# Attention and expert layer on one core: transfers in halves, three at a time, and a scheduler with other costs

## The chip, the core and the metric

The kernel runs on one core of a Trainium2 chip. The metric is the time of one execution on the device in microseconds. The core has a matrix engine (PE, whose weight loads the profile lists as PEld), a vector engine (DVE), an activation engine (ACT), a general engine (POOL) and a sync engine (SP), which here issues nearly all transfers between HBM and the on-chip memory SBUF. Matrix products land in PSUM, which has eight banks. Each engine works through its own list of instructions in order.

## The reference

```python
q_rot, k_rot = (rotate(q), rotate(k))          # 8 batches, 8 heads, 576 rows, 64 columns
scores = scale * np.matmul(q_rot, k_rot.transpose(0, 1, 3, 2))
scores = scores - np.max(scores, axis=-1, keepdims=True)
attn = np.exp(scores)
attn = attn / (np.sum(attn, axis=-1, keepdims=True) + 1e-09)
x = np.matmul(attn, v)                         # then heads side by side: x is (8, 576, 512)
...
scores = np.einsum('bsd,d->bs', x, w_gate)
for b in range(B):
    top_idx = np.argpartition(-scores[b], capacity)[:capacity]     # the 128 best rows of a batch
    xe = x[b, top_idx]
    ye = np.maximum(xe @ w1, 0.0) @ w2                             # 512 to 1024 to 512
    g = 1.0 / (1.0 + np.exp(-scores[b, top_idx]))
    out[b, top_idx] = x[b, top_idx] + g[:, None] * ye              # all other rows are x
```

## The kernel before

Two heads make a pair; four pairs make a batch; there are 32 pairs. For a pair SP loads `k_in` (576 KB), `q_in` (640 KB) and two halves of v in `vt` (576 KB each, v stands four times in it), by `load` (L443) and `load_v` (L459). `k_in` and `q_in` have three buffers, `vt` four (two pairs). POOL rotates k and q by four instructions (`rotate`, L469; the first pair is rotated by DVE). PE multiplies q by k in nine units of 64 or 128 rows, two matmuls each, into two banks per unit (`units`, L508). DVE takes the negative maximum of each row (`nm`), ACT the exponential with the row's sum (`prob`, `sums`), DVE transposes `prob` in 32 x 32 blocks, and PE multiplies by v in two halves of 144 small matmuls (`value`, L556). The result goes through `ot`, is turned by five transposes on PE and is scaled by 1/sum into `x`, on ACT by ten instructions or on DVE by two (`scaled`, L612).

Two pairs fill one half of a batch's `x`. `half_done` (L654) stores it (512 KB and 64 KB), multiplies it by the gate's weights on POOL (`prod`) and sums that up on ACT or DVE (`gp`). `route` (L693) makes the scores `sc`, spreads them over columns by five transposes on PE, counts on DVE how many rows rank ahead (`cnt`, `rank`), and `chosen` selects 128 rows (`sel`), gathers them (`xe`) by an indirect DMA, after which `experts_of` multiplies by `w1t` and `w2t` and scatters the result. The weights' four pieces each (512 KB a piece) are loaded after the products of pairs 0 to 3 (`weights`, L889).

What runs when isn't written by hand. Every step is an `Op` with a key and with durations for the engines that may do it, and `Order.run` (L110) plays through the whole kernel with these numbers: whenever an engine is free, it gets the waiting step with the smallest key whose inputs and banks are there. `issue` (L239) then writes the instructions out in that order. So durations, costs of switching PE between kinds of products (`SWITCH`, `STAY`), the choice of banks (`Banks.take`) and the numbers in `KEY` decide the order of every engine's list, SP's too, but not how long anything takes on the chip. All engine instructions are recorded by one helper, so the profile puts them on one line, L222, and tells them apart by their tiles.

Of the kernel before, what the change touches and what calls it, by code (L numbers as in the profile page):

```python
# [18 lines left out]
P = 128  # L19
# [3 lines left out]
KEY = dict(lag=44704, value=6306, rows=-177, load=43737, rotate=14014, half=1424, gate=72760, route=862,  # L23
           count=116221, select=-5108, turn=109130, step=-36115, hold=2, patience=1011, over=71, narrow=5,
           s01=7594, s02=628, s10=736994, s12=-866157, s20=21404, s21=450)
# [18 lines left out]
class Banks:  # L44
# [13 lines left out]

    def take(self, kind, t):
        f = self.free  # L60
        if kind == "quad":
            i = 0
        elif kind == "wide":
            i = min((max(f[i], f[i + 1]) > t, i < 4, max(f[i], f[i + 1]), i) for i in range(0, self.n, 2))[3]
# [13 lines left out]
class Op:  # L78
    __slots__ = ("engines", "fn", "key", "banks", "waits", "outs", "ready", "start", "end", "done", "mode", "seq", "urgent",
                 "moved")  # L80


class Order:
# [9 lines left out]
    def op(self, engines, fn, key, after=(), bank=None, mode=0, urgent=False, moved=0):  # L93

        o = Op()
        o.moved = moved
# [13 lines left out]
    def run(self):  # L110
# [4 lines left out]
        mode, shared, wire = 0, 0.0, 0.0  # L115
# [13 lines left out]
        while events:  # L129
# [4 lines left out]
            while moved:  # L134
                moved = False
                for e in names:
# [56 lines left out]
                    free[e] = begin + takes  # L193
                    heapq.heappush(events, free[e])
# [44 lines left out]
def issue(tc, nc, order):  # L239

    needs = {}
# [3 lines left out]
    made, last = {}, {}  # L245
# [44 lines left out]
def attention_moe_kernel(ctx: ExitStack, tc: tile.TileContext, q, k, v, w_gate, w1, w2, rope, outs, cap):  # L290
# [152 lines left out]
    def load(pi):  # L443
# [5 lines left out]
        def dma(n, dst, src, use, late, moved):  # L449
            o = op(LOAD, lambda: nc.sync.dma_start(dst, src), key + late, use.before, moved=moved)  # L450
# [3 lines left out]
        for n, use, src, cuts in ("k", kin, k, KCUTS), ("q", qin, q, QCUTS):  # L454
            for i, (lo, hi) in enumerate(zip(cuts, cuts[1:]) if pi == 0 else [(0, cuts[-1])]):
                dma(n, use.tile[:, :, lo:hi], src[b, j, :, :, lo:hi], use, 2 * i + (n == "q"), 8 * P * (hi - lo))
        loaded[pi] = (kin, qin, got)

    def load_v(pi):  # L459
        b, j = divmod(pi, NP)  # L460
        vals[pi] = []
        for i in range(2):
            use, src = vts.next(), v[b, j, :, i * NB // 2:(i + 1) * NB // 2]
            o = op(LOAD, lambda use=use, src=src: nc.sync.dma_start(use.tile, src),
                   at(pi, 0) - KEY["load"] + 5 + i, use.before, moved=8 * P * NB // 2 * D)
            use.by(o)
            vals[pi].append((use, o))
# [32 lines left out]
    def attend(pi):  # L500
# [7 lines left out]
        def units(us, key):  # L508
# [16 lines left out]
            o = op(pe(2 * M288 + 24 * (len(us) - 1)), products, key, needs + room, bs,  # L525
# [30 lines left out]
        def value(key, late):  # L556
# [17 lines left out]
            for i in range(2):  # L574
                o = op(pe(NB // 2 * 280), lambda i=i: products(i), key, turned + [got[i], o], acc, mode=1)
# [19 lines left out]
            gd = op({"ACT": act(9, 60.0)}, guarded, key, list(exps.values()) + rs.before)  # L595
            rr = op({"DVE": dve(9, 1, 60.0)}, lambda: nc.vector.reciprocal(r, r), key, [gd])
# [23 lines left out]
            g = op({"DVE": dve(4 * P), "ACT": act(4 * P, 7 * 40.0)},  # L620
# [4 lines left out]
            g_ = op({"DVE": dve(P), "ACT": act(P, 40.0)},  # L625
# [28 lines left out]
    def half_done(b, i, key):  # L654
# [4 lines left out]
        s0 = op(STORE, lambda: nc.sync.dma_start(outs[b][0:512, cs].rearrange("(p t) m -> p t m", t=NT), x.tile[:, 0:4, :]),  # L659
                key, made, moved=4 * P * NT * DM // 2)  # L660
        s1 = op(STORE, lambda: nc.sync.dma_start(outs[b][512:S, cs], x.tile[0:REM, 4, :]), key, made,
                moved=2 * REM * DM)
# [3 lines left out]
        for t0, t1 in () if b == B - 1 and i else ((0, 2), (2, 4), (4, 5)):  # L666
# [16 lines left out]
            o = op({"DVE": dve((t1 - t0) * DM // 2), "ACT": act((t1 - t0) * DM // 2, (t1 - t0) * 247.0 - 40.0)},  # L683
# [5 lines left out]
        x.by(s0, s1)  # L689
        stored += [s0, s1]  # L690
# [309 lines left out]
```

## Time and profile before

| | us |
|---|---|
| median of 3 runs | 618.16 (614.37 to 623.51) |
| profiled execution | 617.93 |
| its span, first to last instruction | 616.2 |
| PE busy | 536.7 (87%) |
| DVE busy | 469.6 (76%) |
| ACT busy | 353.8 (57%) |
| POOL busy | 353.4 (57%) |

97.91 MB pass the DMA engines in the span, 159 GB/s on average. The granted PE clock is 0.983 of full speed on average. In rows of the trace PE products are named by what they read: `k_in,q_in` is q times k, `prob,vt` the value product, `ident,...` a transpose, `xt,w1t` and `w2t,ht` the experts. "Idle before" with a releaser is time in which that engine stood still until the named engine's work ended; "issue" there means that nothing the profile shows was waited for.

### The profile page before, as it was taken

What the parts mean: (1) busy time and instruction counts of PE and PEld (TensorE: products, weight loads), DVE (VectorE), ACT (ScalarE), POOL (GpSimd) and SP (SyncE); (2) the same over time, 40 slices, a digit from 0 to 9 for tenths busy, and PEclk for the clock granted to TensorE, in tenths of its full rate; (3) what the DMA queues carried; (4) which work ended last, traced back from release to release, by engine and by line L of the source; (5) the groups of instructions that cost most, each with busy time, mean ns of one, the idle gap of its engine ahead of it and who ended that gap; (6) DMA issues with size and microseconds to landing.
All of it is one profiled execution on the core that took longest, in us unless ns stands there. A gap on an engine that the chain in (4) does not pass through costs nothing.

```text
span 616.2 us, 25530 instructions
## 1 busy us (share of the span) xinstructions
PE 536.7 (87%) x11280; PEld 386.5 (63%) x11280; DVE 469.6 (76%) x849; ACT 353.8 (57%) x1121; POOL 353.4 (57%) x271
## 2 busy tenths in 40 slices
PE   4777977787879998899988999899988999899996
PEld 2445755565657755677567675577566775577673
DVE  6967877979889967898679876899578976895420
ACT  3555756655766655665665745666566656763300
POOL 2948586457666835577553938568464867122110
PEclk9899898999989999899999999999998999999999
DMA  8756655453635464253555444454654534230110
GB/s 322 279 196 260 211 194 183 161 161 135 210 118 190 161 213 165 90 173 131 197 178 195 165 124 148 144 183 155 215 176 139 164 117 176 81 118 21 40 52 17
DMA packets 32974, 97.91 MB, mean 159 GB/s; under 512 B 3040, under 2 KB 14048, under 8 KB 32864
## 3 DMA queue, kind: packets, MB, share of 16 engines
q1 hardware_dynamic: 31040, 91.50, 43.4%
q0 software_dynamic: 1280, 4.20, 2.0%
q8 instruction: 88, 1.44, 0.9%
q10 hardware_dynamic: 544, 0.59, 0.3%
q14 instruction: 22, 0.18, 0.1%
HBM read 84.74 MB, written 11.53 MB: 156 GB/s over the span
## 4 chain that ended last, share of the span: by engine, by line
PE 56%; DVE 15%; ACT 11%; issue 8%; POOL 5%; DMA 4%; POOLq 0%; DVEq 0%; SPq 0%
PE banks L222 56%; ACT prob L222 7%; DVE nm L222 7%; DVE prob L222 6%; DMA k_in<-k_dram 4%; ACT x L222 3%; POOL k_in L222 2%; POOL q_in L222 1%; POOL prod L222 1%; DVE junk L222 1%; ACT row L222 0%; DVE k_in L222 0%; POOL out_dram L222 0%; ACT prod L222 0%; DVE q_in L222 0%
## 5 line engine op out<-in xcount | busy, mean ns | idle before, releaser
L222 ACT ACTIVATE prob<-banks,nm 128x576 f32<-128x576 f32 x288 | 211.2, 739 | 166.2 <-DVE nm L222 165.6
L222 DVE TENSOR_REDUCE nm<-banks 128x1 f32<-128x576 f32 x288 | 204.0, 747 | 65.4 <-PE banks L222 62.7
L222 PE MATMUL banks<-k_in,q_in 64*128 64x288 f32 (+1 forms) x1152 | 207.2, 451 | 36.6 <-ACT prob L222 19.0
L222 DVE STREAM_TRANSPOSE prob<-prob 128x1152 f32<-128x1152 f32 (+1 forms) x160 | 194.6, 1236 | 22.3 <-ACT prob L222 22.3
L222 PE MATMUL banks<-prob,vt 32*64 32x160 f32 (+1 forms) x9216 | 189.0, 295 | 25.7 <-issue 16.3
L222 PEld LDWEIGHTS banks<-prob,vt 32*64 32x64 f32 x9216 | 161.7, 131 | 57.8 <-issue 35.2
L222 PEld LDWEIGHTS banks<-k_in,q_in 64*128 64x128 f32 (+1 forms) x1152 | 118.5, 198 | 103.6 <-ACT prob L222 30.5
L222 POOL TENSOR_TENSOR k_in<-k_in,tabk 128x1152 f32<-128x1152 f32 x31 | 81.5, 2628 | 158.2 <-DMA k_in<-k_dram 125.0
L222 POOL TENSOR_TENSOR q_in<-q_in,tabq 128x1280 f32<-128x1280 f32 x31 | 89.9, 2901 | 0.8 <-DMA q_in<-q_dram 0.8
L222 POOL TENSOR_TENSOR prod<-x,wg 128x512 f32<-128x512 f32 (+1 forms) x45 | 48.8, 1102 | 38.8 <-DVE x L222 22.5
L222 PEld LDWEIGHTS banks<-xt,w1t 128*128 128x128 f32 x512 | 59.4, 192 | 7.3 <-issue 5.7
L222 PE MATMUL banks<-xt,w1t 128*128 128x128 f32 x512 | 63.9, 280 | 0.0
L222 PE MATMUL banks<-w2t,ht 128*128 128x512 f32 x128 | 60.6, 602 | 0.8 <-ACT ht L222 0.6
L222 ACT ACTIVATION_READ_ACCUMULATOR prob<-banks,nm 128x1 f32 x288 | 57.5, 200 | 0.0
L222 POOL TENSOR_TENSOR q_in<-q_in 128x640 f32<-128x640 f32 x31 | 47.8, 1543 | 0.1
L222 ACT ACTIVATE x<-banks,rs 128x64 f32<-128x64 f32 (+1 forms) x196 | 42.8, 328 | 6.0 <-PE banks L222 5.5
L222 POOL TENSOR_TENSOR k_in<-k_in 128x576 f32<-128x576 f32 x31 | 43.7, 1410 | 0.0
L222 ACT COPY ot<-banks 64x64 f32<-64x64 f32 (+1 forms) x93 | 27.4, 328 | 21.1 <-PE banks L222 20.8
L222 ACT ACTIVATE prod<-prod 128x256 f32<-128x256 f32 (+1 forms) x70 | 28.5, 408 | 17.0 <-POOL prod L222 16.9
L222 DVE TENSOR_SCALAR_CACHE_REDUCE junk<-row,sc 128x128 bf16<-128x128 f32 (+8 forms) x72 | 36.2, 528 | 1.3 <-ACT row L222 1.1
L222 PEld LDWEIGHTS banks<-w2t,ht 128*128 128x128 f32 x128 | 22.2, 190 | 22.7 <-issue 19.6
L222 PE MATMUL banks<-ident,ot 128*128 128x128 f32 (+1 forms) x160 | 23.6, 279 | 8.5 <-ACT prob L222 8.5
(61 smaller groups left out, 204.0 us busy)
## 6 DMA issues: line engine op xcount, KB each, us to landing
vt<-v_dram SPq DMA_DIRECT2D x64, 576.0 KB, 4.8
q_in<-q_dram SPq DMA_DIRECT2D x31, 640.0 KB, 7.3
k_in<-k_dram SPq DMA_DIRECT2D x31, 576.0 KB, 6.1
out_dram<-x SPq DMA_DIRECT2D x16, 512.0 KB, 3.4
w1t<-w_dram SPq DMA_DIRECT2D x4, 512.0 KB, 6.6
w2t<-w_dram SPq DMA_DIRECT2D x4, 512.0 KB, 7.4
out_dram<-x SPq DMA_DIRECT2D x16, 64.0 KB, 3.0
tabk<-rope_dram ACTq DMA_DIRECT2D x2, 288.0 KB, 4.3
```

The costliest lines, as they stand in the source:

```text
L222: i = made(*args, **kwargs)
```

## The change

Loads of k and q after the first two pairs, of v after the first pair, and of the weights are cut in halves, and the main store in two. These, and the small store, are marked `alone`. In the written program each of them waits until the third before it has landed; in the scheduler's play SP isn't free for another step before that time either. Besides, `KEY`, `SWITCH` and several durations have other numbers, and the choice of banks has two new settings.

```diff
-KEY = dict(lag=44704, value=6306, rows=-177, load=43737, rotate=14014, half=1424, gate=72760, route=862,
+KEY = dict(tnear=2, wnear=0, lag=47626, value=10910, rows=18240, load=16004, rotate=-168669, half=-4551,
...
-SWITCH = ((0.0, 175.0, 194.0), (151.0, 0.0, 196.0), (151.0, 125.0, 0.0))
+SWITCH = ((0.0, 95.0, 196.0), (200.0, 0.0, 200.0), (150.0, 260.0, 0.0))
+DEPTH = 3
...
+    def far(self, i, near):
+        return near < 2 and (i < 4) != (near == 1)
...
-            i = min((i < 4, f[i ^ 1] <= t, f[i], i) for i in range(self.n) if f[i] <= t)[3]
+            i = min((self.far(i, KEY["tnear"]), f[i ^ 1] <= t, f[i], i) for i in range(self.n) if f[i] <= t)[3]
...
+                    if o.alone:
+                        free[e] = max(free[e], landed[-1] + self.SEM)
+                        landed = [o.end] + landed[:-1]
...
+        if o.alone:
+            if len(transfers) >= DEPTH:
+                tc.add_manual_dep(
+                    mine[0], transfers[-DEPTH], mybir.DependencyInfo(mybir.DependencyClass.Sync, mybir.DependencyReason.DATA),
+                    reason="transfers at a time")
+            transfers.append(mine[-1].name)
...
-            for i, (lo, hi) in enumerate(zip(cuts, cuts[1:]) if pi == 0 else [(0, cuts[-1])]):
+            for i, (lo, hi) in enumerate(zip(cuts, cuts[1:]) if pi == 0 else ()):
                 dma(n, use.tile[:, :, lo:hi], src[b, j, :, :, lo:hi], use, 2 * i + (n == "q"), 8 * P * (hi - lo))
+            for i in range(2 if pi else 0):
+                dma(n, use.tile[:, i], src[b, j, :, i], use, 2 * (n == "q") + i, 4 * P * cuts[-1])
...
+            for n, (c0, c1) in enumerate(((0, NB // 4), (NB // 4, NB // 2))):
+                o = op(LOAD, lambda use=use, src=src, cs=slice(c0, c1): nc.sync.dma_start(use.tile[:, cs], src[:, cs]),
+                       at(pi, 0) - KEY["load"] + 5 + 2 * i + n, use.before, moved=8 * P * (c1 - c0) * D, alone=pi > 0)
...
-            g = op({"DVE": dve(4 * P), "ACT": act(4 * P, 7 * 40.0)},
+            g = op({"DVE": dve(4 * P), "ACT": (8 * 205, 8 * 205 + 120)},
...
-            o = op({"DVE": dve((t1 - t0) * DM // 2), "ACT": act((t1 - t0) * DM // 2, (t1 - t0) * 247.0 - 40.0)},
+            o = op({"DVE": dve((t1 - t0) * DM // 2), "ACT": act((t1 - t0) * DM // 2, (t1 - t0) * 160.0 - 20.0)},
```

On SP, around the second pair's products, the list before has whole transfers (a name is tile and buffer, the shape is what lands in SBUF):

```order
L222 DMA k_in0_78<-k_dram 128x1152
L222 DMA q_in0_75<-q_dram 128x1280
L222 DMA w1t_120<-w1_dram 128x1024
L222 DMA w2t_121<-w2_dram 128x2x512
L222 DMA vt0_81<-v_dram 128x1152
L222 DMA w1t_120<-w1_dram 128x1024
L222 DMA w2t_121<-w2_dram 128x2x512
L222 DMA vt1_82<-v_dram 128x1152
```

and the list of the change, from the same load of `k_in0` on:

```order
L233 DMA k_in0_78<-k_dram 128x576 x2
L233 DMA q_in0_75<-q_dram 128x640 x2
L233 DMA vt0_81<-v_dram 128x512
L233 DMA vt0_81<-v_dram 128x640
L233 DMA w1t_120<-w1_dram 128x512 x2
L233 DMA w2t_121<-w2_dram 128x512
L233 DMA vt1_82<-v_dram 128x512
L233 DMA vt1_82<-v_dram 128x640
L233 DMA w2t_121<-w2_dram 128x512
```

Each transfer is now two, a group of weights (the first stands further ahead) follows v's first half instead of leading it, and v's second half goes between the pieces of w2.

On PE, where the scores of batch 3 are transposed (`sc`), the list before has this between the value products of two pairs (one row of q times k with x4 is two units):

```order
L222 MATMUL banks_63<-k_in0_78,q_in0_75 128x288 x4
L222 MATMUL banks_63<-ident_64,sc0_106 128x128 x5
L222 MATMUL banks_63<-ident_64,ot0_88 128x128 x4
L222 MATMUL banks_63<-ident_64,ot0_88 64x128
L222 MATMUL banks_63<-k_in0_78,q_in0_75 128x288 x10
```

and the list of the change, at the same scores:

```order
L233 MATMUL banks_63<-k_in0_78,q_in0_75 128x288 x4
L233 MATMUL banks_63<-ident_64,sc0_106 128x128 x5
L233 MATMUL banks_63<-w2t_121,ht0_103 128x512 x2
L233 MATMUL banks_63<-ident_64,ot0_88 128x128 x4
L233 MATMUL banks_63<-ident_64,ot0_88 64x128
L233 MATMUL banks_63<-w2t_121,ht0_103 128x512 x2
L233 MATMUL banks_63<-k_in0_78,q_in0_75 128x288 x4
L233 MATMUL banks_63<-w2t_121,ht0_103 128x512 x2
L233 MATMUL banks_63<-k_in0_78,q_in0_75 128x288 x4
L233 MATMUL banks_63<-w2t_121,ht0_103 128x512 x2
L233 MATMUL banks_63<-k_in0_78,q_in0_75 128x288 x4
```

The four pieces of the second expert product stood one pair earlier before and are now spread between these; two of q times k more come here as well.

## Rows read from the trace of the kernel before

**Rows 1.** The page: engines' busy time (share), and the chain that ended last.

```profile
PE 536.7 (87%) x11280; PEld 386.5 (63%) x11280; DVE 469.6 (76%) x849; ACT 353.8 (57%) x1121; POOL 353.4 (57%) x271
PE 56%; DVE 15%; ACT 11%; issue 8%; POOL 5%; DMA 4%; POOLq 0%; DVEq 0%; SPq 0%
```

**Rows 2.** Busy time in stretches: length, engines (instructions), PE clock, DMA share, GB/s.

```profile
20.00:180.00 160.00, 123.76 (x3008) 89.55 (x3008) 130.21 (x212) 100.61 (x322) 109.86 (x72) 0.96 0.56 190
180.00:570.00 390.00, 362.03 (x8012) 263.65 (x8012) 314.05 (x548) 237.11 (x760) 230.29 (x178) 0.99 0.45 151
570.00:616.20 46.20, 39.99 (x224) 27.36 (x224) 11.83 (x58) 7.64 (x21) 5.12 (x9) 1.00 0.10 36
```

**Rows 3.** Waits of PE from 0 to 180 us: total, times, longest.

```profile
PE banks L222 <- ACT prob L222: 17.8, 22, 2.3
PE banks L222 <- issue: 12.8, 7, 2.9
...
PE banks L222 <- ACT x L222: 3.4, 3, 1.8
```

**Rows 4.** The page's DMA queues: packets, MB, share of 16 engines.

```profile
q8 instruction: 88, 1.44, 0.9%
```

**Rows 5.** Timeline of SP, 30 to 38 us: start, duration, what it issued.

```profile
30.92 0.34 SPq L222 DMA_DIRECT2D vt<-v_dram  x1
31.30 0.43 SPq L222 DMA_DIRECT2D w1t<-w_dram  x1
31.78 0.43 SPq L222 DMA_DIRECT2D w2t<-w_dram  x1
```

**Rows 6.** Timeline of PE, 28 to 38 us; in brackets the idle time before.

```profile
37.49 0.49 PE L222 MATMUL banks<-prob,vt 32*64 32x160 f32 x6 [2.88 <-issue]
```

**Rows 7.** DMA traffic from 31.8 to 35.2 us, and from 35.2 to 37.5.

```profile
DMA packets 278, 1.11 MB, mean 325 GB/s; under 512 B 21, under 2 KB 21, under 8 KB 278
...
q8 instruction: 1, 0.02, 2.7%
```

**Rows 8.** Timeline of SP, 300 to 420 us.

```profile
328.56 0.33 SPq L222 DMA_DIRECT2D k_in<-k_dram  x1
```

**Rows 9.** Timeline of POOL, 336 to 350 us.

```profile
336.25 2.64 POOL L222 TENSOR_TENSOR k_in<-k_in,tabk 128x1152 f32<-128x1152 f32 x1 [9.30 <-DMA k_in<-k_dram]
...
346.26 1.54 POOL L222 TENSOR_TENSOR q_in<-q_in 128x640 f32<-128x640 f32 x1
```

**Rows 10.** Timeline of PE, 346 to 350 us.

```profile
348.58 1.67 PE L222 MATMUL banks<-k_in,q_in 64*128 64x288 f32 x10
```

**Rows 11.** The page's DMA issues: count, KB each, median us to landing.

```profile
k_in<-k_dram SPq DMA_DIRECT2D x31, 576.0 KB, 6.1
...
out_dram<-x SPq DMA_DIRECT2D x16, 64.0 KB, 3.0
```

**Rows 12.** Timeline of PE at the scores of batch 3, and of batch 4.

```profile
316.61 0.76 PE L222 MATMUL banks<-ident,sc 128*128 128x128 f32 x5
...
318.90 1.24 PE L222 MATMUL banks<-k_in,q_in 128*128 128x288 f32 x4 [0.99 <-ACT prob L222]
320.90 1.24 PE L222 MATMUL banks<-k_in,q_in 64*128 64x288 f32 x8 [0.76 <-ACT x L222]
...
324.59 2.73 PE L222 MATMUL banks<-prob,vt 32*64 32x160 f32 x144 [1.01 <-ACT prob L222]
...
387.29 0.76 PE L222 MATMUL banks<-ident,sc 128*128 128x128 f32 x5
```

**Rows 13.** Groups by shape: count, busy us, mean ns, idle before and its releaser.

```profile
L222 DVE TENSOR_TENSOR x<-banks,rs 128x512 f32<-128x512 f32 x14 | 9.4, 674 | 0.0
L222 DVE TENSOR_REDUCE gp<-prod 64x1 f32<-64x256 f32 x5 | 2.1, 411 | 8.7 <-POOL prod L222 8.7
L222 DVE TENSOR_TENSOR x<-banks,rs 64x128 f32<-64x128 f32 x6 | 1.6, 273 | 8.2 <-PE banks L222 8.2
```

**Rows 14.** Timeline of PE at the end.

```profile
570.57 2.05 PE L222 MATMUL banks<-xt,w1t 128*128 128x128 f32 x16
...
577.72 1.88 PE L222 MATMUL banks<-w2t,ht 128*128 128x512 f32 x4
579.44 0.27 PE L222 MATMUL banks<-ident,sc 128*128 128x128 f32 x1
```

More of the change, by code (lines that the diff above doesn't have):

```diff
@@ L79 @@
     __slots__ = ("engines", "fn", "key", "banks", "waits", "outs", "ready", "start", "end", "done", "mode", "seq", "urgent",
-                 "moved")
+                 "moved", "alone")
 class Order:
@@ L91, in __init__, with op @@
         self.ops, self.slots = [], slots
-    def op(self, engines, fn, key, after=(), bank=None, mode=0, urgent=False, moved=0):
+    def op(self, engines, fn, key, after=(), bank=None, mode=0, urgent=False, moved=0, alone=False):
         o = Op()
-        o.moved = moved
+        o.moved, o.alone = moved, alone
         o.urgent = urgent
@@ L114, in run @@
         free = {e: 0.0 for e in names}
-        mode, shared, wire = 0, 0.0, 0.0
+        mode, shared, wire, landed = 0, 0.0, 0.0, [0.0] * (DEPTH - 1)
         waiting = {e: [] for e in names}
@@ L244, in issue @@
             needs.setdefault(id(n), []).append(o)
-    made, last = {}, {}
+    made, last, transfers = {}, {}, []
     for _, _, o, e in order:
@@ L449, in dma @@
         def dma(n, dst, src, use, late, moved):
-            o = op(LOAD, lambda: nc.sync.dma_start(dst, src), key + late, use.before, moved=moved)
+            o = op(LOAD, lambda: nc.sync.dma_start(dst, src), key + late, use.before, moved=moved, alone=pi > 1)
             use.by(o)
@@ L463, in load_v @@
             use, src = vts.next(), v[b, j, :, i * NB // 2:(i + 1) * NB // 2]
[L464 to L467, printed above, removed]
+            got = []
+            for n, (c0, c1) in enumerate(((0, NB // 4), (NB // 4, NB // 2))):
+                o = op(LOAD, lambda use=use, src=src, cs=slice(c0, c1): nc.sync.dma_start(use.tile[:, cs], src[:, cs]),
+                       at(pi, 0) - KEY["load"] + 5 + 2 * i + n, use.before, moved=8 * P * (c1 - c0) * D, alone=pi > 0)
+                got.append(o)
+            use.by(*got)
+            vals[pi].append((use, got))
     def rotate(pi):
@@ L593, in guarded @@
                 nc.scalar.add(r[0:64, U:U + 1], su[64:128, 8:9], EPS)
-            gd = op({"ACT": act(9, 60.0)}, guarded, key, list(exps.values()) + rs.before)
-            rr = op({"DVE": dve(9, 1, 60.0)}, lambda: nc.vector.reciprocal(r, r), key, [gd])
+            gd = op({"ACT": (320, 425)}, guarded, key, list(exps.values()) + rs.before)
+            rr = op({"DVE": dve(9, 1, 20.0)}, lambda: nc.vector.reciprocal(r, r), key, [gd])
             sums.by(gd)
@@ L624, in value @@
                    key + late, [f, rr] + x.before, b)
-            g_ = op({"DVE": dve(P), "ACT": act(P, 40.0)},
+            g_ = op({"DVE": dve(P), "ACT": (2 * 205, 2 * 205 + 120)},
                     lambda e: scaled(e, x.tile[0:REM, 4:5, cs].rearrange("p t (h d) -> p t h d", h=2),
@@ L779, in select @@
                         sel.tile[:, t, :], slots[:, r0 // P], rank.tile[:, t:t + 1], None, op0=ALU.is_equal)
-        s = op({"DVE": dve(P, 5, 350.0), "POOL": (5 * (60 + 2.38 * P), 5 * (60 + 2.38 * P))}, select, key, [rk_] + sel.before)
+        s = op({"DVE": dve(P, 5, 350.0), "POOL": (5 * 589, 5 * 589)}, select, key, [rk_] + sel.before)
         rank.by(s)
@@ L843, in part @@
                         nc.tensor.matmul(bank_of(bank)[:, out], lhs, rhs, start=first, stop=last)
-                o = op(pe(sum(max(T32, M512 / 2 * (m[0].stop - m[0].start) / 512) * 2 for m in mms)), part,
+                o = op(pe(sum(max(T32 + 4, M512 / 2 * (m[0].stop - m[0].start) / 512) * 2 for m in mms)), part,
                        key + (step // 2 if i else 0), needs + [o], bank)
```

36 lines of the change are left out of this document (22 added, 14 removed).

## The prediction, on record before the change was run

> **What bounds the kernel now.** I began with the page's chain of waits: over half of it is PE and 8% is "issue", time in which nothing that the profile shows was waited for [rows 1]. PE's matmul order is therefore the thing to follow, and the question is where it stands still. The busy times by stretch answer that [rows 2]: between 180 and 570 us PE is busy 362.03 of 390 us (93%), DVE 314.05 (81%); between 20 and 180 us PE is busy 123.76 of 160 (77%) and DVE 130.21 (81%), so neither bounds that stage and PE stands for 36 us. The last 46 us are a chain of routing and experts. PE's waits before 180 us [rows 3] name the parts: softmax results (ACT prob) 17.8 us, "issue" 12.8 us in 7 stops, ACT's scaling of the output rows (ACT x) 3.4 us.
>
> What is an "issue" stop? The queue table has an instruction queue that moved 1.44 MB in 88 packets [rows 4], about 16 KB each; PE and its weight loads are 22,560 instructions, 256 to a packet, so these are PE's program arriving in blocks over the same DMA engines as the data. Now the longest stop: SP issues a v load, a w1 piece and a w2 piece within 0.9 us, 576 + 512 + 512 = 1600 KB by the page's sizes [rows 5]; PE stops in the middle of a value product, 6 matmuls short, and goes on at 37.49 after 2.88 us [rows 6]. Between 31.8 and 35.2 us data alone moved, 278 packets at 325 GB/s; the one packet of the instruction queue comes in the stretch behind it [rows 7]. So the block of instructions waited for the burst to drain.
>
> **The change, part by part.** The sum goes against the profiled execution, 617.93 us (a span of 616.2 and 1.7 around it); the median of the three runs is 618.16, 0.2 above.
>
> *Transfers in halves, three at a time.* Three halves are 768 to 960 KB, typically 864. At 325 GB/s [rows 7] 1600 KB need 5.0 us to drain and 864 KB 2.7, so a block that waits behind a full burst is 2.3 us earlier. That is as long as all but the longest of the 7 stops of rows 3, and would leave 1 us or so of 12.8. Since blocks meet a load more often when the same bytes are spread out, I take **10 us** off; the ends are 0 and 12.8. This is the first 180 us alone, where the order of SP's loads changes most (first listing above): the weights' four groups are interleaved with v loads in pieces.
>
> By the Trainium skill ("DMA: Bandwidth & Descriptors", section "Queues, rings and completion order") a DMA engine goes round-robin between its queues packet by packet, and by "Runtime: NRT & Kernel Launch", section "Instruction fetch mechanics", fetching is hidden since dispatch is slower than the refill. Both speak against this term and would make it 0, 10 us more in the sum; rows 6 and 7 speak against them here, and the first rival carries them.
>
> The halves also let the rotation start sooner. A k load is issued at 328.56 [rows 8] and POOL starts on it at 336.25; POOL ends the pair's rotation at 347.80 [rows 9] and PE's first product that can use it starts at 348.58 [rows 10], 0.8 us of slack, so this path decides in some pairs: DMA is 4% of the chain [rows 1], 25 us with the first load. Both halves of k now go ahead of q. k alone, 576 KB at 325 GB/s, is 1.8 us on top of the 3.0 us that even a 64 KB store takes to land [rows 11]: 4.8 instead of 7.7. That is up to 2.9 us in about three places of the chain; POOL has the sums of the gate (prod) to do in between, so I take **3**; ends 0 and 9. In 18 of the pairs the second half of q is put behind both halves of a v load; POOL's multiplication and addition on k cover 4 us of that.
>
> *The order on PE.* Once per batch of four pairs PE has transposes of scores and output and then five units of q·k with nothing between them: stops of 0.99, 0.76 and 1.01 us [rows 12]. The change puts the second expert product there in four pieces (second listing); it does so in 5 of the 7 places, since the first two batches have no experts yet. 5 x 2.76 = 13.8 us if all is gained. But the expert work has left another pair, which now has none, and PE waits for softmax there instead: before the experts begin, from 20 to 180 us, DVE has more to do than PE [rows 2]. I take half, **7**; ends 0 and 13.8.
>
> *ACT or DVE.* The scheduler now has ACT's scaling at 8 x 205 ns and gives DVE 24 large and 32 small ones, where it had 14 and 6. DVE gains 10 x 674 + 26 x 273 ns = 13.8 us [rows 13], spread over 550 us in which it is idle for 106 [rows 2]: beside other work. PE's waits for ACT x fall, **2** of the 3.4 in rows 3 (those in the middle stage are in the term before). DVE also gets ten more sums of the gate, 15 for 5. The five cost 2.1 us of work and 8.7 us of standing still until POOL's product came [rows 13], with every row maximum queued behind them on DVE and ACT and PE behind those. Ten more at that price would be 21.6 us; but eight of them come in pairs, or stand where the product is done early, and DVE has room. I add **3**; ends 0 and 21.6.
>
> *The end.* Of the expert work that PE did after the last value product, one piece of w1 (2.05 us) and one of w2 (1.88) are now ahead of it [rows 14]: 3.9 us more before it. Behind it these two filled PE while scores were ranked, and the last transpose of scores waited for one of them, from 577.72 to 579.44; it now goes with the other four. I count **+2.5**; ends 0 and 3.9. The kernel's start has the same order of loads up to pair 1 and is taken as equal. Bank choice, switch costs and the other durations have no price but the order that they make.
>
> Sum: 617.9 - 10 - 3 - 7 - 2 + 3 + 2.5 = 601.4, say **601 us**.
>
> **Rivals.** *The stops stay.* If a block of instructions waits for something other than the amount queued (three transfers are still always ahead of it), the first term is 0: 611 us. For it: the change never empties the queue, it only shortens it. Against it: rows 5 to 7. Chance 0.14.
>
> *The stops move.* The order removes holes, and DVE, with 20 us more work and in-order waits for POOL, opens others: the third term 0 and DVE's +10 instead of +3, 601.4 + 14 = 615 us. For it: between 20 and 570 us DVE already has more to do than ACT and POOL. Chance 0.16.
>
> *Loads become the pace, slower.* SP's queue is in order, and each transfer now holds it until the third before has landed. A pair takes (387.29 - 316.61)/4 = 17.7 us [rows 12] and needs 8 halves and 1.5 stores. Three at a time do that if one lands within 17.7/9.5 x 3 = 5.6 us of its issue; from there on loads decide. The nearest rows are 3.0 us (64 KB store) and 6.1 (a k load of twice the size, beside q) [rows 11]. At 3.0 + 0.9 for its own 288 KB it is 3.9, and 70% of a pair. At 6.1 it would be 19.3 us for a pair, 1.6 more, over the 22 pairs from 180 to 570 us 35 us: 636 us. Chance 0.12. The Trainium skill ("DMA: Bandwidth & Descriptors", "Rules for kernel authors") asks for at least 1 MiB in a DMA for full bandwidth, and is on this rival's side.
>
> *Everything at its good end.* -12.8 - 9 - 13.8 - 3.4 + 0 + 0 would be 579; half of the way there from the forecast is 590. Chance 0.08.
>
> **How the numbers follow.** The forecast has the remaining 0.50, with 594 to 609 as its own range. 2% of 618 is 12.4 us, about what a measurement of this kernel can tell from no change (the three runs span 9.1 us): faster is under 605.8, slower over 630.5. Four fifths of the forecast, the good end and a little of the first two rivals are faster: 0.40 + 0.08 + 0.05 = 0.53. Slower is the third rival and a remnant, 0.13; the rest, 0.34, is within. The range reaches from 587, leaving out half of the good end, to 618, which takes in the first two rivals and leaves out the third: 0.16 outside.
>
> **What would show it.** PE's "issue" waits before 180 us at 1 to 4 us for 12.8, and none over 1 us; PE busy over 83% from 20 to 180 us. k to POOL in 5 to 6 us instead of 7.7. No stops of 0.76 us behind ACT x after the scores' transposes, and a period of four pairs of 68 to 70 us instead of 70.7. DVE busy 485 to 495 us. The same 45 us from the last value product to the end. Wrong if "issue" is still over 9 us, if POOL starts later than 7.7 us after k's issue and PE stands behind it, or if DVE stands for more than 15 us behind POOL prod.

## The result: 1.0% faster, a third of what was forecast

| | before | after |
|---|---|---|
| median of 12 runs each, us | 617.64 (614.37 to 623.51) | 611.60 (607.33 to 618.97) |
| profiled execution, its span | 617.93, 616.2 | 607.33, 605.6 |

The ratio is 0.9898 (0.9859 to 0.9937). Measured twice more, beside other kernels and on another chip, it was 0.9858 (0.9780 to 0.9936) and 0.9875 (0.9834 to 0.9917). So the change is 6 to 9 us faster, where 16.5 were forecast. Ratios set fast runs against fast runs; for e8, e9 and e11 below, on whose chip the record counts seven of the thirteen runs of the kernel before as slow, the other six would give 0.992, 0.995 and 0.976 in place of the 0.984, 0.987 and 0.968 on record. The profiled execution of after is the shortest of its twelve, 4.3 us under its median, and its difference to before, 10.6 us, is larger than that of the medians.

The profile of after, read in the order of the prediction. First the page: engines and chain (answers to [rows 1]).

```profile
PE 529.1 (87%) x11280; PEld 380.5 (63%) x11280; DVE 486.5 (80%) x898; ACT 318.8 (53%) x948; POOL 355.6 (59%) x271
PE 67%; DVE 12%; issue 9%; ACT 8%; POOL 1%; DMA 1%; POOLq 0%; SPq 0%; DVEq 0%
```

POOL and DMA have all but left the chain (1% each, for 5% and 4%), PE has 67% for 56%; "issue" has not gone down. PE's idle time is span less busy: 79.5 us before, 76.5 after. The other 7.6 of the 10.6 us are busy time of the same 11,280 products. Part of that belongs to this execution, not to the kernel. Until PE's last product the granted clock was 0.50 (1.2 GHz instead of 2.4) for 20.5 us in before and for 10.2 in after, which is worth at most 5.1 us; two later profiles of the same kernel have 23.9 us of it and PE busy 534.0 and 533.8 us, at a mean clock of 0.979, where this one has 0.989. One such stretch of after, in PE's timeline beside the same work at full clock, and its busy times (the 0.50 is the clock):

```profile
192.49 0.50 PE L233 MATMUL banks<-prob,vt 32*64 32x128 f32 x8 [1.75 <-issue]
192.92 3.90 PE L233 MATMUL banks<-k_in,q_in 64*128 64x288 f32 x16
...
265.28 2.37 PE L233 MATMUL banks<-k_in,q_in 64*128 64x288 f32 x16
```

```profile
193.10:196.30 3.20, 3.20 (x14) 2.29 (x16) 1.13 (x2) 1.18 (x4) 2.62 (x1) 0.50 0.78 217
```

PE had just stood for 1.75 us. The busy times by stretch (answers to [rows 2], columns as there):

```profile
20.00:180.00 160.00, 130.80 (x3328) 94.30 (x3328) 145.25 (x238) 94.17 (x281) 118.03 (x75) 0.98 0.67 209
180.00:570.00 390.00, 360.23 (x7746) 260.24 (x7743) 317.14 (x581) 211.24 (x639) 225.38 (x179) 1.00 0.48 147
```

Before 180 us PE gained 7 us, 82% busy for 77%. From 180 to 570 us it gained nothing: 360.23 for 362.03. Why not, its waits tell: of after from 0 to 180 us (answers to [rows 3]) ...

```profile
PE banks L233 <- ACT prob L233: 19.8, 24, 1.8
...
PE banks L233 <- issue: 6.1, 8, 1.6
...
PE banks L233 <- ACT x L233: 0.8, 2, 0.4
```

... and from 180 to 560 us, of before and then of after:

```profile
PE banks L222 <- ACT prob L222: 19.3, 28, 1.5
PE banks L222 <- issue: 4.0, 11, 1.7
PE banks L222 <- ACT x L222: 3.0, 4, 0.8
```

```profile
PE banks L233 <- issue: 17.2, 27, 2.0
PE banks L233 <- ACT prob L233: 9.8, 16, 0.8
PE banks L233 <- ACT rs L233: 1.5, 2, 0.8
PE banks L233 <- ACT ht L233: 0.7, 1, 0.7
```

The new order removed 12.5 us of standing behind ACT prob and ACT x (22.3 to 9.8) and brought 2.2 us behind other work of ACT (`rs` and `ht`). "Issue" grew by 13.2 there, so that PE stands 2.9 us more in this stage than before. PE's timeline of after, from 240 to 320 us:

```profile
242.16 1.06 PE L233 MATMUL banks<-prob,vt 32*64 32x160 f32 x46 [0.53 <-issue]
...
264.82 0.53 PE L233 MATMUL banks<-prob,vt 32*64 32x160 f32 x16 [1.97 <-issue]
...
300.51 0.76 PE L233 MATMUL banks<-ident,sc 128*128 128x128 f32 x5
301.10 1.88 PE L233 MATMUL banks<-w2t,ht 128*128 128x512 f32 x4
302.82 0.75 PE L233 MATMUL banks<-ident,ot 128*128 128x128 f32 x5
...
313.16 1.06 PE L233 MATMUL banks<-prob,vt 32*64 32x160 f32 x46 [0.53 <-issue]
```

At the scores, where [rows 12] had three holes, expert pieces follow without a gap. The three rows with "issue" are new stops. That at 264.82 is of the kind of [rows 6]: 16 matmuls short of a group's end, behind loads that SP's timeline shows just ahead of it:

```profile
258.01 1.71 SPq L233 DMA_DIRECT2D vt<-v_dram  x2
260.54 0.80 SPq L233 DMA_DIRECT2D k_in<-k_dram  x2
262.19 0.33 SPq L233 DMA_DIRECT2D q_in<-q_dram  x1
```

Which stops are blocks of the program can be counted. Take PE's instructions in the order of the trace: products, weight loads, and the hundred or so semaphore instructions among them. In all twenty profiles of this document every "issue" stop of PE over 0.55 us stands at the same place in 256, at a count of 191 to 194 past a multiple of 256. So these are beginnings of blocks. Of after's 17.2 us from 180 to 560 us 12.5 stand there, of its two later profiles' 20.4 and 22.0 us 17.8 and 19.4, and of before's 4.0 us 1.9.

The stop of 0.53 us at 242.16 and 313.16 is another. It comes once in each of five batches, 71 to 72 us apart (three more follow), ahead of the same value product and at other counts. The new order has it in every profile, 2.6 us in all, and the old order in none; what PE waits for there no row says. Blocks come back nearly as regularly: PE's 22,560 products and weight loads in eight batches are 2,820 for a batch, 11.02 blocks of 256, so a block begins at almost the same place of every batch. But one that comes late in one batch need not come late in the next: the 1.97 us of 264.82 have no like a batch later.

The rest of what the prediction looked for. A k load to POOL's start on it (answers to [rows 8, 9]), SP's timeline and then POOL's: 4.9 us, and 3.7 to 5.7 in its neighbours, for 7.7.

```profile
368.14 0.80 SPq L233 DMA_DIRECT2D k_in<-k_dram  x2
...
373.01 2.63 POOL L233 TENSOR_TENSOR k_in<-k_in,tabk 128x1152 f32<-128x1152 f32 x1 [4.44 <-DMA k_in<-k_dram]
```

DVE's groups by shape (answers to [rows 13]): no sum of the gate waits for POOL.

```profile
L233 DVE TENSOR_REDUCE gp<-prod 128x2 f32<-128x512 f32 x9 | 6.0, 672 | 0.0
L233 DVE TENSOR_REDUCE gp<-prod 64x1 f32<-64x256 f32 x6 | 2.4, 401 | 0.0
```

And the end (answers to [rows 14]): from the last output transposes of the seventh batch on, PE's timeline of before ...

```profile
511.28 0.71 PE L222 MATMUL banks<-ident,ot 128*128 128x128 f32 x5
```

... and of after:

```profile
498.40 0.77 PE L233 MATMUL banks<-ident,ot 128*128 128x128 f32 x5 [0.61 <-ACT prob L233]
...
563.88 1.98 PE L233 MATMUL banks<-w2t,ht 128*128 128x512 f32 x4
```

After's last value product ends where the last of these rows begins. From the first transposes to the last value product it was 59.3 us and is 65.5, and from there to the end 45.6 and now 41.7.

### The profile page after: what moved, and what is told of

The parts are those of the page before. It is cut to its first block, busy times and chain, and to the rows that moved or that the text cites. A ratio compares the mean times of both kernels' runs of the same rounds, so it can differ in the third digit from the quotient of the medians.

```text
span 605.6 us, 25663 instructions
## 1 busy us (share of the span) xinstructions
PE 529.1 (87%) x11280; PEld 380.5 (63%) x11280; DVE 486.5 (80%) x898; ACT 318.8 (53%) x948; POOL 355.6 (59%) x271
## 4 chain that ended last, share of the span: by engine, by line
PE 67%; DVE 12%; issue 9%; ACT 8%; POOL 1%; DMA 1%; POOLq 0%; SPq 0%; DVEq 0%
PE banks L233 67%; ACT prob L233 7%; DVE nm L233 6%; DVE prob L233 3%; DVE junk L233 2%; DMA q_in<-q_dram 1%; POOL q_in L233 1%; DVE x L233 1%; ACT x L233 0%; DVE sel L233 0%; POOL k_in L233 0%; DVE q_in L233 0%; POOLq L1023 0%; DVE k_in L233 0%; POOL xe L233 0%
## 5 line engine op out<-in xcount | busy, mean ns | idle before, releaser
L233 PE MATMUL banks<-k_in,q_in 64*128 64x288 f32 (+1 forms) x1152 | 199.8, 438 | 29.2 <-ACT prob L233 11.6
L233 PE MATMUL banks<-prob,vt 32*64 32x128 f32 (+1 forms) x9216 | 188.3, 293 | 27.2 <-issue 21.6
L233 DVE STREAM_TRANSPOSE prob<-prob 128x1152 f32<-128x1152 f32 (+1 forms) x160 | 193.2, 1234 | 11.9 <-ACT prob L233 11.9
L233 PEld LDWEIGHTS banks<-k_in,q_in 64*128 64x128 f32 (+1 forms) x1152 | 113.8, 192 | 95.8 <-ACT prob L233 31.0
L233 POOL TENSOR_TENSOR prod<-x,wg 128x512 f32<-128x512 f32 (+1 forms) x45 | 48.6, 1101 | 14.6 <-DVE x L233 12.5
L233 POOL DMA_INDIRECT out_dram<-xe,idx x8 | 8.5, 1059 | 49.2 <-DVE xe L233 48.0
L233 PE MATMUL banks<-ident,ot 128*128 128x128 f32 (+1 forms) x160 | 24.4, 282 | 13.5 <-ACT prob L233 13.2
L233 PEld LDWEIGHTS banks<-ident,ot 128*128 128x128 f32 (+1 forms) x160 | 16.1, 135 | 27.8 <-ACT prob L233 26.5
```

The costliest lines, as they stand in the source:

```text
L233: i = made(*args, **kwargs)
```

## Experiments

Three questions: where the new stops come from (the cap, v's bytes, all data, or the order), what each half of the change is worth alone, and whether a third version beats both kernels. All ratios are to the kernel before on the same chip. "Holes" are PE's waits for ACT prob and ACT x from 180 to 560 us.

**The cap and v's bytes.** e1 takes the wait away and leaves order and halves.

```diff
-            if len(transfers) >= DEPTH:
+            if len(transfers) >= 100000:
```

> The change's own order and halves, word for word, without the wait for the third transfer before. Two theories of why PE's issue stops grew from 4.7 to 17.2 us behind 180 us while they shrank from 12.8 to 6.1 us ahead of it. Theory A (spread): halves under the cap keep the data queue occupied more of the time, so more instruction blocks meet a load; without the cap, issue behind 180 us falls to 8 us or less, ahead of 180 us it rises to 10 or more, and the time is 607 to 612 us. Theory B (order): the new PE list puts value products closer together, so PE uses up its blocks faster than they come; without the cap, issue behind 180 us stays at 14 us or more and ahead of it rises to 10 or more, and the time is 613 to 620 us.

617.42 us, ratio 0.9912 (0.9872 to 0.9952). PE's waits from 180 to 560 us:

```profile
PE banks L233 <- issue: 26.2, 23, 3.0
PE banks L233 <- ACT prob L233: 10.0, 16, 0.8
```

More stops without the cap (26.2 us, for 17.2 to 22.0 in three profiles of the change), so the cap doesn't bring them; it seems to take some away. e2 and e3 load only a slice of v from the third pair on (products use what is there), in the order after and in that of before.

```diff
-cs=slice(c0, c1)
+cs=slice(c0, c1 if pi < 2 else c0 + 1)
```

> The change with v loads that bring a ninth to a quarter of their bytes from the third pair on (the rest of the tile keeps the values of an earlier pair, so the result is another); order, waits and number of transfers stay. If stops for instructions come from data ahead of them in the queue, PE's issue total falls from 23.3 to 10 us or less and the time by 8 to 14 us, to 597 to 604 us. If they come from the pace of PE's own program (a limit that no data is part of), issue stays over 18 us and the time falls by 3 us at most.

> The kernel before with v loads that bring a ninth of their bytes from the third pair on (the result is another). What all contention with v is worth in the old order: if the stops are due to data in the queue, issue falls from 18.0 to 9 us or less and the time by 6 to 12 us, to 606 to 612 us; if not, issue stays over 14 us and the time falls by 2 us at most.

e2: 611.05 us, 0.9798 (0.9739 to 0.9857), issue 20.6 us behind 180 us. e3: 616.02, 0.9898 (0.9846 to 0.9950), issue 7.8. The traces move 70.4 and 66.5 MB for 97.9, about 30% less, and that takes no stop away in either; it is not v in particular. Both are 0.6 to 1% faster than with the whole of v all the same, and these runs do not show by what.

**One half of the change at a time.** e4 has halves, cap and DEPTH in the scheduler, with the keys, switch costs, durations and bank choice of before.

```diff
-SWITCH = ((0.0, 95.0, 196.0), (200.0, 0.0, 200.0), (150.0, 260.0, 0.0))
+SWITCH = ((0.0, 175.0, 194.0), (151.0, 0.0, 196.0), (151.0, 125.0, 0.0))
...
```

> Halves, cap and the scheduler that knows of it, with the numbers, durations and bank choice of before. Theory A (spread): issue behind 180 us is 12 us or more in an order much like the old one, ahead of 180 us it is 8 or less; the time is 613 to 620 us. Theory B (order): issue behind 180 us is 7 us or less, ahead of it 8 or less; the time is 604 to 611 us, better than the whole change.

663.03 us, 1.0678 (1.0618 to 1.0737): the scheduler, played anew with the old keys, makes another order, whose holes are 38.5 us. That says nothing of halves; it shows that old keys belong to old transfers. e5 is the converse, new numbers with whole and unlimited transfers (k, q, v, weights and stores); from 60 us on its PE order is that of after.

```diff
-            for i in range(2 if pi else 0):
+            for i in range(0):
```

> The new keys, switch costs, durations and bank choice alone; transfers whole and unlimited, as before. Theory B (the new order of PE is what brings the stops behind 180 us, halves and cap take some of them away again): issue at least 25 us behind 180 us and 35 in all, as without the cap, and 616 to 622 us, so that the transfers' part of the change is worth 5 to 10 us. Theory C (halves themselves make more blocks of instructions meet a load): issue under 10 us behind 180 us, as in the kernel before, and 600 to 608 us.

642.63 us, 1.0317 (1.0239 to 1.0396). PE's waits from 180 to 560 us:

```profile
PE banks L233 <- issue: 34.5, 24, 3.5
PE banks L233 <- ACT prob L233: 11.2, 14, 3.0
```

The theory that the order brings the stops holds, and costs more than it expected; halves are not their source but what makes this order bearable. Not all of the cost is stops: against the change's profile on the same chip (a2, below) PE stands 17.4 us more in "issue" (42.2 for 24.8) and is busy 7.4 us more (541.4 for 534.0), with 40.9 us for 23.9 at a granted clock of 0.50. With e5, the change itself was run again (a2):

> The changed kernel once more, unedited, so that the three kernels beside it have it on the same chip. Both theories: ratio to the kernel before 0.985 to 0.995, PE 'issue' about 6 us before 180 us and 15 to 20 us behind it. If its issue total lies more than 6 us from the 23.3 of its first profile, single profiles can't carry differences of that size.

613.73 us, 0.9858 (0.9780 to 0.9936); issue 3.8 us before and 20.4 behind 180 us.

e8 does halves and cap alone as they ought to be done: the kernel before, row by row in its order on PE, DVE, ACT and POOL, only that each load emits two transfers in its place.

```diff
-            o = op(LOAD, lambda: nc.sync.dma_start(dst, src), key + late, ...
+            o = op(LOAD, lambda: each(*[lambda i=i: nc.sync.dma_start(dst[:, i], src[:, i]) for i in range(2)]), ...
...
+        for i in mine:
+            if len(transfers) >= CAP: tc.add_manual_dep(i, transfers[-CAP], ...)
+            transfers.append(i.name)
```

> The kernel before with its own order on every engine, row by row; only each transfer (k, q from the second pair, v, weights, stores) goes as two in the same place of SP's order, and from the third pair on each waits for the third before it. This is the first term of the prediction by itself. If halves and cap shorten the stops of any order: issue before 180 us falls from 12.8 to under 5, behind it stays near 4.7, and the time is 606 to 612 us on the first chip's scale, ratio 0.980 to 0.990. Theory I (they only repair what the new order makes; the old order has few stops to repair and meets the cap's waits): issue 13 us or more in all, ratio 0.992 to 1.005. Rival (SP held in this order): PE and POOL wait for k, q or v, ratio over 1.01.

> The same without the wait: halves alone in the old order. In the new order halves without the wait already gave most (whole transfers 642.6, halves without the wait 617.4, with it 611 to 614, on different chips). If that holds in the old order too, the ratio is within 0.007 of the run with the wait, and issue at most 4 us above it. If the wait is what counts here, issue before 180 us is 8 us or more above it.

e8: 613.70 us, 0.9844 (0.9792 to 0.9896); e9, without the cap: 614.84, 0.9868 (0.9796 to 0.9941). What the wait itself gives in this order can't be told from these two. The kernel before ran between 612.42 and 630.13 us on their chip, so what e8 is worth is read from it once more, on one chip with the change:

> Halves and cap in the old order, unedited, again: ratio 0.980 to 0.990, issue about 3 us before 180 us and 10 to 14 behind it.

> The changed kernel, unedited, beside halves and cap in the old order on the same chip. If the new order is worth the 6.5 us predicted beside the first term: 0.009 to 0.012 under the ratio of the other. If its gain is eaten by stops and by the longer end: within 0.005 of it. Issue 20 to 25 us in all.

612.27 us, 0.9859 (0.9814 to 0.9903), and the change 614.66, 0.9875 (0.9834 to 0.9917). PE's waits of e8's second run, from 0 to 180 us and from 180 to 560:

```profile
PE banks L230 <- ACT prob L230: 18.1, 25, 2.3
...
PE banks L230 <- issue: 5.6, 8, 1.8
PE banks L230 <- ACT x L230: 3.3, 3, 1.8
...
PE banks L230 <- ACT prob L230: 17.1, 25, 1.0
PE banks L230 <- issue: 7.9, 9, 1.3
PE banks L230 <- ACT x L230: 3.8, 5, 0.8
```

So halves and cap alone give what the whole change gives; the new order adds nothing that can be measured, though it has 11 us of holes less. The two profiles account for that: PE is busy 533.8 us in the change and 533.9 in e8's second run, and stands in "issue" for 27.8 us in the change and 14.3 in the other.

**Is it data?** e6 (order after) and e11 (order before) load only 32 columns of k and q from the fourth pair on, and a slice of v; e6 has halves and the wait, e11 whole transfers.

```diff
+                w = cuts[-1] if pi < 3 else 32
-                dma(n, use.tile[:, i], src[b, j, :, i], ...
+                dma(n, use.tile[:, i, :w], src[b, j, :, i, :w], ...
```

> The changed kernel, but k and q loads from the fourth pair and v loads from the third bring only a small part of their data (the products then use what earlier pairs left); orders, waits and number of transfers stay. Theory D (blocks of instructions wait behind data of any kind): from 180 to 560 us issue falls from 17.2 to under 4 us, PE busy over 95% there, 592 to 600 us. Theory P (PE in this order simply runs its program faster than blocks arrive, data or not): issue stays over 14 us, 606 to 611 us.

> The kernel before, but k and q loads from the fourth pair and v loads from the third bring only a small part of their data; order and number of transfers stay. With the thin loads in the new order (0.960) this tells what the new order alone is worth where little data stands ahead of PE's program. If the holes that the new order fills are worth the 9 to 14 us that were predicted: 606 to 612 us, ratio 0.972 to 0.983, waits for ACT prob and ACT x behind 180 us at 20 us as before. If the new order is worth nothing in itself: ratio 0.960 to 0.967.

e6: 598.61 us, 0.9600 (0.9524 to 0.9675). e11: 604.12, 0.9682 (0.9629 to 0.9735). PE's waits from 180 to 560 us, of e6 and then of e11:

```profile
PE banks L233 <- issue: 10.2, 18, 1.3
PE banks L233 <- ACT prob L233: 10.0, 16, 0.7
```

```profile
PE banks L222 <- ACT prob L222: 17.6, 26, 1.0
PE banks L222 <- issue: 6.9, 9, 1.5
PE banks L222 <- ACT x L222: 3.8, 5, 0.8
```

Both theories of e6 are half right: 7 to 12 us of the stops are data, 10 stay without it, 2.6 of them the stop that is no block's beginning. With the bytes away, the new order is 0.8% ahead of the old (5 us) by the ratios; they are of two chips and their intervals overlap, so the size isn't settled. Its holes are 11.4 us less, its stops 3.3 more, and at beginnings of blocks 7.6 for 6.9 us, nearly the same. With all the bytes they are 19.4 us in the change and 7.9 in e8's second run: data before the blocks cost the new order more than the old, and that is what eats its gain.

**Fewer bytes ahead.** e7 lets two halves be under way instead of three; e10 four quarters, the same bytes in four pieces.

```diff
-            if len(transfers) >= DEPTH:
+            if len(transfers) >= 2:
```

> The changed kernel in the same order, but a transfer waits for the second before it instead of the third: two halves under way, 576 KB at most for k or q. Theory D: a block of instructions waits behind 576 KB instead of 864, 0.9 us less at 325 GB/s; with 20 or so stops behind 180 us issue falls to 8 us or less there, and the time to 600 to 606 us. Rival (loads become the pace): 9.5 transfers in 17.7 us need one each 1.86 us, so two at a time need a landing within 3.7 us of the issue; the halves landed in 3.4 to 4.1. Then PE, DVE and POOL wait for DMA, issue falls all the same, and the time is 615 to 635 us.

> The changed kernel in its own order, with k, q and v in quarters from the third pair on and a transfer waiting for the fourth before it: 576 to 640 KB under way, as with two halves, but in four pieces. Theory D (the data ahead of a block sets the length of a stop): issue behind 180 us falls from 17 to 20 to about 14, as with two halves (13.7). Whether the pace holds: each quarter has to land in 17.7/17.5 x 4 = 4.0 us; the halves took 3.4 to 4.1 with three under way, 16 KB ones 1.8 to 2.0, so about 2.8 is expected and the first 180 us have no waits for POOL q_in beyond the one at the start. Then 604 to 611 us, ratio 0.972 to 0.985. Rival (SP's issue of twice as many transfers, or the weights' pieces between them, hold the loads up): waits for POOL q_in over 8 us before 180 us and a ratio over 0.995.

e7: 628.73 us, 1.0099 (1.0027 to 1.0171). Its issue behind 180 us is 13.7 us, but PE's waits from 0 to 180 us are

```profile
PE banks L233 <- ACT prob L233: 24.9, 19, 8.4
PE banks L233 <- POOL q_in L233: 14.0, 4, 6.5
```

In the stage where the weights come too, two at a time are too few: the prediction's third rival, there and not after. Its halves landed in 3.1 to 3.5 us, within the 3.7 that a steady pair allows. e10: 623.27, 1.0075 (1.0021 to 1.0130), issue 18.2 behind 180 us and 8.3 us behind POOL q_in before it. With 576 to 640 KB ahead as in e7, it has the stops of three halves (17.2 to 22.0 us) and not the 13.7 of e7. That speaks against the amount alone, but one profile of each is little: profiles of one program differ by as much.

**Why so few in the old order?** e12 has halves and cap only for the first ten pairs, the weights and two batches' stores (`EARLY = 10`), whole transfers after that. e13 is the kernel before with 64 small matmuls ahead, while PE waits for its first data; they were meant to move every block's start by 128 instructions.

```diff
+    for n in range(64):
+        nc.tensor.matmul(banks[0:32, 7, 0:32], ident[:, 0:32], ident[:, 0:32], start=True, stop=True)
     issue(tc, nc, order.run())
```

> The old order with halves and cap only for the first ten pairs, all weights and the first two batches' stores, that is about the first 180 us; whole transfers from there, as in the kernel before. If halves are what meets more blocks behind 180 us: issue 3 to 5 us before and 4 to 6 behind it, 8 us less than with halves throughout, ratio 0.970 to 0.978, faster than the change. Rival (the old kernel's few stops there rest on where its blocks fall against the loads, and PE now comes 5 us earlier): issue over 10 us behind 180 us, ratio 0.982 to 0.995.

> The kernel before with 64 small matmuls and their weight loads (32x32) put ahead of PE's first product, while PE waits 7.5 us for its first data anyway: every block of 256 instructions then begins 128 instructions earlier in the work, and nothing else moves. If the 4 to 5 us of issue behind 180 us rest on where the blocks begin: issue there 9 us or more, and 4 to 10 us slower (ratio 1.006 to 1.016). If the length of the bursts alone counts: issue within 3 us of 18 in all, ratio 0.996 to 1.004.

e12: 615.12 us, 0.9888 (0.9836 to 0.9941), issue 10.0 us behind 180 us, with the very loads that had 4.0 in before: its rival came true. e13: 624.00, 1.0026 (0.9992 to 1.0061), issue 11.3. But it did not move the blocks. In the trace each of the 64 calls is two products and two weight loads, 256 instructions in all, which is one whole block, and the instruction queue has 89 packets for 88 (PE's groups by shape; the page's DMA queues):

```profile
L222 PE MATMUL banks<-ident 128*32 128x32 f32 x128 | 6.4, 231 | 1.4 <-POOL ident masks.py:199 1.4
```

```profile
q8 instruction: 89, 1.46, 1.0%
```

So the blocks begin at the same products as in before. One stop in PE's timeline of before, and the same in e13's:

```profile
148.71 0.29 PE L222 MATMUL banks<-prob,vt 32*64 32x160 f32 x1 [1.20 <-issue]
```

```profile
152.91 0.29 PE L222 MATMUL banks<-prob,vt 32*64 32x160 f32 x1 [1.20 <-issue]
```

And a stop that e13 has in three batches stands at the same products as in e12, which has nothing put ahead; PE's timeline of e12 and then of e13:

```profile
383.47 0.49 PE L230 MATMUL banks<-prob,vt 32*64 32x128 f32 x4 [1.84 <-issue]
```

```profile
393.10 0.49 PE L222 MATMUL banks<-prob,vt 32*64 32x128 f32 x4 [1.84 <-issue]
...
464.62 0.52 PE L222 MATMUL banks<-prob,vt 32*64 32x160 f32 x12 [1.84 <-issue]
...
535.91 0.76 PE L222 MATMUL banks<-prob,vt 32*64 32x128 f32 x20 [1.74 <-issue]
```

So e13 is the kernel before once more, with PE's first product of q times k 0.4 us later (7.92 for 7.54). Its 11.3 us and e12's 10.0 show that the 4.0 us of before's one profile are not given by its order, its loads and its blocks; with all three the same, this stage has had 4.0 to 11.3 us. What a shift of the blocks would do no run shows. The time hardly moved: 7.3 us more of stops in the middle stage went with 1.6 us (0.5 less to 3.8 more) by the ratio.

**A version that beats both?** e15 (new order) and e16 (old order) have three under way up to the tenth pair and two behind it; `alone` is now the number, for v and stores likewise.

```diff
-alone=pi > 1
+alone=0 if pi < 2 else 3 if pi < 10 else 2
```

> The changed kernel in its own order; three transfers under way up to the tenth pair, for the weights and for the first two batches' stores, two from there. With two throughout, all of the loss (22 us) was made before 180 us, and from there to the end of the seventh batch it took 282.8 us against 284.7 to 291.2 for the change. If the amount under way sets the stops: issue behind 180 us 13 to 15 us instead of 17 to 22, ratio 0.978 to 0.985, and this beats the change. If a shorter burst only moves PE's wait to the products behind the loads: ratio within 0.005 of 0.9875.

> Halves in the old order, with the same two caps. By the first theory: issue behind 180 us 6 to 8 us instead of 8 to 12, ratio 0.979 to 0.984. By the second: 0.982 to 0.990, as with three.

e15: 613.38 us, 0.9926 (0.9890 to 0.9961); e16: 614.69, 0.9959 (0.9926 to 0.9992), on a chip where the kernel before takes 618.73. Issue behind 180 us is down as the first theory expected, to 12.2 and 5.8 us, and no gain comes of it. Neither has a better ratio than the change, which was not run on this chip. In e15, issue before 180 us is 9.5 us, where the same program up to there had 3.8 to 6.1: single profiles of one schedule differ by that much.

All of it in one table: ratio; issue and holes from 180 to 560 us.

| transfers | old order | new order |
|---|---|---|
| whole, no cap | 1; 4.0 (e13 11.3); 22.3 | 1.0317; 34.5; 11.2 |
| halves, no cap | 0.9868; 10.3; 18.7 | 0.9912; 26.2; 10.0 |
| halves, three | 0.9844, 0.9859; 11.9, 7.9; 20.3, 20.9 | 0.9898, 0.9858, 0.9875; 17.2, 20.4, 22.0; 9.8, 9.3, 9.7 |
| halves, two behind 180 us | 0.9959; 5.8; 21.8 | 0.9926; 12.2; 11.0 |
| little data | 0.9682; 6.9; 21.4 | 0.9600; 10.2; 10.0 |

## Why the prediction was wrong, by its steps

The sign was right, the size was not: -16.5 forecast, -6 to -9 measured.

- **Halves, three at a time (-10), and the k path (-3).** Before 180 us issue fell from 12.8 to 6.1 us (3.8 and 5.2 in the other profiles), 6.7 to 9.0 us less for the 10 forecast; the signs named, 1 to 4 us and no stop over 1 us, were not quite met (the longest is 1.6). The prediction's 2.3 us are not as long as all but the longest of the seven stops, as it says, the second being 2.53; the 1 us that it leaves comes out all the same. The step that failed is its limit, "This is the first 180 us alone": the stops behind 180 us were left at the 4.0 us of one profile, as if they belonged to the place, and are 17 to 22. In the old order they are 8 to 12 with halves, and 10.0 and 11.3 with whole loads behind 180 us (e12, e13), so that not even there was 4.0 a sure base. Halves and cap alone are worth 1.4% (9 us) beside the change, both terms together, not 13. The k path did become as short as forecast (3.7 to 5.7 us for 5 to 6), POOL and DMA all but left the chain, and no run shows a gain of its own from that.
- **The order on PE (-7).** The holes went further than I dared to say: 12.5 of at most 13.8 us (10.3 with the 2.2 us of new waits for ACT), and the pair without experts doesn't wait for softmax (no hole is over 0.8 us). But I asked only what stands in the hole, not what is late next. It was the next block of the program, and the period of four pairs came out at 71 to 72 us, where 68 to 70 were forecast for 70.7. The table shows it in every row: the new order has 9 to 11 us less of holes, and at equal transfers 3 to 30 us more of issue. Side by side, the whole change came out 0.0016 (1 us) slower than halves and cap alone. For what it has beside them -3.5 us were forecast, which lies at the edge of what the two intervals, 0.004 to each side, allow.
- **ACT or DVE (-2, +3).** ACT x before 180 us fell by 2.6 us, for 2 forecast; 1.5 us of it came back as waits for DVE (`x` 0.9, `rs` 0.6). The sums of the gate wait for nothing, +3 was 0. DVE is busy 486.5 us, in the forecast's 485 to 495.
- **The end (+2.5).** 6.2 us more to the last value product and 3.9 less behind it, +2.3; in the other two profiles +1.1 and +1.7. The size was right, the sign that should have shown it ("the same 45 us") was not.
- In after's profile PE's waits from 0 to 180 us are 3.8 us less in all (issue -6.7, ACT x -2.6, ACT prob +2.0, the second pair's rotation +2.3, others +1.2), from 180 to 560 us 2.9 more (-12.5, +2.2 and +13.2, as above) and behind that 1.8 less: -2.7. The end's +2.3 is no term beside these; its stretch holds some of the same waits. PE's busy time is 7.6 us less, much of it that one execution's clock, and the two make most of the 10.6.
- **Rivals.** The time is that of "the stops stay", the mechanism nearer to "the stops move", with PE's program in DVE's place. "Loads become the pace" was excluded by its own point, 3.4 to 4.1 us landing for 5.6, and e7 shows that it is real one step further.

"Instruction fetch mechanics" in the Trainium skill ("Runtime: NRT & Kernel Launch") has fetching hidden. The profiles here have 18.0, 23.3 and, in e5, 42.2 us of issue stops on PE, of which 15.6, 18.3 and 39.6 us stand at beginnings of blocks, so that measurement decides against it. The Trainium skill's rule of at least 1 MiB for a DMA ("DMA: Bandwidth & Descriptors", "Rules for kernel authors") is one for full bandwidth. As a rule for the time it would speak against halves, and e8's second run has them 1.4% faster.

Not settled: how much of the gain is the clock. Beside each other on one chip, the kernel before has a mean granted clock of 0.974, the change 0.984, and halves and cap alone (e8's second run) 0.983. As an estimate from these, PE is at 1.2 GHz for 11 to 13 us less of the span, which is worth up to some 6 of the 8 or 9 us. Whether fewer stops keep the clock up, no run separates.

That PE, standing less behind softmax, reaches the end of a block sooner fits all rows, but no run varied that alone. Nor is it known why fewer stops in e16, and more in e13, move the time so little.

## What to carry to other kernels

A hole that is filled on the busiest engine is worth what the next wait leaves of it; look for that wait in all stages, not only where the change touches the queue. Where a long unrolled program streams in beside the data, price an order and a transfer size together: here each of the two alone, with its keys not fitted to it, was 3 to 7% slower, while cutting the transfers in the untouched order gave the whole gain. And a stage with few stops in one profile may have more in the next: profile it again before a forecast leaves them where they are. Count in the trace what an edit puts into a queue: the 64 calls of e13 were 256 instructions, so the shift that they were meant to make did not happen.

## What the runs showed of the hardware

- PE's stops for its program stand at one place in 256 of its instructions: in twenty profiles every "issue" stop over 0.55 us is at a count of 191 to 194 past a multiple of 256. In e12 and in e13 one of them comes back in three batches, 11 blocks on each time (1.84, 1.84 and 1.74 us in e13).
- Sixteen products of q times k took 2.37 us at a granted clock of 1.00 and 3.90 us in a stretch at 0.50 (1.2 GHz), ahead of which PE had stood for 1.75 us.
- One fp32 matmul call is two products and two weight loads on PE (e13: 64 calls, 128 of each).
- Single profiles of one program differ by 5 us in the stops of one stage (3.8 to 9.5 before 180 us, 17.2 to 22.0 behind it) and in PE's busy time (529.1 to 534.0), so a difference of profiles is held against medians.
- Halves of 256 to 320 KB landed in 2.5 to 4.1 us with three under way, 3.1 to 3.5 for k, q and v with two; quarters of 128 to 192 KB with four under way in 2.8 to 3.3.
